# Wv in chunks, x0 in one transfer, the swapped Wv over GpSimd's queue: loads rearranged in a gated mix of linear attention and an MLP

## The chip, the cores and the metric

The kernel runs on one core of one Trainium2 chip. The metric is the device time of one execution in microseconds. Before the change it took 156.04 us (median of 3 runs, 155.99 to 156.21). The span in a profile, from the first to the last instruction, is 1.7 us shorter than the time of the same execution (154.9 us beside 156.61 for the first profile).

## The reference, cut to what matters

x has 2048 rows of 448. One branch is linear attention with 16 heads of 28: q, k and v are projections of x, q and k pass a per-head matrix and a pair of softmaxes, and the products are summed over the sequence. The other branch is a GELU MLP with 1792 hidden units. A sigmoid gate of x mixes both.

```python
g = _sigmoid((x * gate_w).sum(-1, keepdims=True))
qkv = (x @ wqkv) ...                       # wqkv is 448 x 1344: Wq, Wk, Wv side by side
pq = einsum("bhsd,hdf->bhsf", q, w_phi)    # the same for k
phi_q = concat([softmax(pq), softmax(-pq)])
...                                        # kv and z are sums over the sequence; o = num / den
b = einsum("bsf,fd->bsd", gelu(einsum("bsd,df->bsf", x, w1) + b1), w2) + b2
return g * (o @ wo) + (1 - g) * b
```

Of the kernel before, what the change touches and what calls it, by code (L numbers as in the profile page):

```python
# [13 lines left out]
D = 448  # L14
# [3 lines left out]
P = 128  # L18
# [5 lines left out]
NJ = 14  # L24
# [4 lines left out]
HP = 64  # L29
# [6 lines left out]
def kernel(  # L36
# [14 lines left out]
    nc = tc.nc  # L51
    x = A_x[0]
# [16 lines left out]
    def four(name):  # L69
        turn[0] += 1  # L70
        return wide(name) if turn[0] % 4 == 0 else pair(name)
# [26 lines left out]
    WvG = attn.tile([P, NC4, D + 1], BF16, name="WvG")  # L98
    WvS = attn.tile([P, NC4, D + 1], BF16, name="WvS")
# [4 lines left out]
    WkT = attn.tile([P, NG, D], BF16, name="WkT")  # L104
    WqT = attn.tile([P, NG, D], BF16, name="WqT")
    wphi = attn.tile([P, NC4, DH], BF16, name="wphi")
# [4 lines left out]
    b1c = w2_sb[:, 6, 0:P]  # L111
    nc.gpsimd.memset(b1c, 0.0)
    warm = w2_sb[:, 0, 0:P]
    gate = w2_sb[:, 1, :]
# [3 lines left out]
    nc.vector.memset(WvG[0:64, 3, :], 0.0)  # L118
    nc.vector.memset(wo_sb[64:P, 3, :], 0.0)
    nc.vector.memset(Wpk[0:64, 3, :], 0.0)  # L120
    nc.vector.memset(WkT[0:1, 0, 0:1], 0.0)
    wphi_rows = A_w_phi.rearrange("h a b -> (h a) b")
    x0 = oT[:, 0, 0:4 * D].rearrange("p (t d) -> p t d", t=4)
    for m, eng in ((0, nc.scalar), (1, nc.sync)):
        eng.dma_start(x0[:, 2 * m:2 * m + 2, :],
                      x[m * 256:(m + 1) * 256, :].rearrange("(t p) d -> p t d", p=P))
    nc.scalar.dma_start(WvG[:, 0:3, 0:D],
                        A_wqkv[0:384, 2 * D:3 * D].rearrange("(c p) n -> p c n", p=P))
    nc.scalar.dma_start(WvG[64:P, 3, 0:D], A_wqkv[384:448, 2 * D:3 * D])
    nc.sync.dma_start(gate[0:1, :], gate_w[None, :])  # L130
    nc.scalar.dma_start(wphi[:, 0:3, :], wphi_rows[0:384, :].rearrange("(c p) b -> p c b", p=P))

    def load_x(b):
        blk = slice(b * 512, (b + 1) * 512)
        nc.sync.dma_start_transpose(xT[:, 0:3, blk], x[blk, 0:384])  # L135
        nc.sync.dma_start_transpose(xT[:, 3, blk], x[blk, 320:448])  # L136
# [4 lines left out]
    def swap_x(h):  # L141
        ev = slice(2 * h * 512, 2 * h * 512 + 512)
        od = slice(2 * h * 512 + 512, 2 * h * 512 + 1024)
        nc.sync.dma_start(xS[0:HP, :, h, :], xT[HP:P, :, ev])  # L144
        nc.sync.dma_start(xS[HP:P, 0:3, h, :], xT[0:HP, 0:3, od])
# [1 line left out]
    load_wT(WkT, D)  # L147
    load_wT(WqT, 0)
    load_x(1)
    nc.scalar.dma_start(wphi[0:64, 3, :], wphi_rows[384:448, :])  # L150


    first = consts.tile([1, 1], F32, name="first")
# [1 line left out]
    nc.gpsimd.memset(ident[:], 1.0)  # L155
    nc.gpsimd.affine_select(out=ident[:], in_=ident[:], pattern=[[-1, P]],
                            compare_op=ALU.is_equal, fill=0.0, base=0, channel_multiplier=1)
    nc.gpsimd.memset(hmask[:], 1.0)
    nc.gpsimd.affine_select(out=hmask[:], in_=hmask[:], pattern=[[P, NC4], [-DH, H]],
                            compare_op=ALU.is_ge, fill=0.0, base=0, channel_multiplier=1)  # L160
# [14 lines left out]
                          in_=mask[:, PW:PW + 2, None].to_broadcast([P, 2, DH]))  # L175
    nc.gpsimd.memset(KVbd[:], 0.0)
    for g in range(NG):
        nc.gpsimd.tensor_copy(
            out=KVbd[:, g].rearrange("p s (i w) -> p s i w", i=2)[:, :, :, KW - 2:KW],
            in_=m4[:, None, :, :].to_broadcast([P, 2, 2, 2]))  # L180
# [36 lines left out]
    def prep(W_T, out_at, engines):  # L217
        for m in range(2):
            w_ps = four("w_ps")
            for i in range(2):  # L220
                c = 2 * m + i
                dlo = c * P if c < 3 else 320
                for e, (h0, h1) in enumerate(spans):
                    nc.tensor.matmul(w_ps[:, i, h0 * DH:h1 * DH], lhsT=W_T[:, e, dlo:dlo + P],
                                     rhs=bd[:, e, h0:h1, :].rearrange("p h d -> p (h d)"),
                                     start=(e == 0), stop=(e == NC4 - 1), skip_group_check=True)
            src = w_ps[:, :, 0:D].rearrange("p i (x w) -> p i x w", w=PW)
            if m == 0:
                copy(engines[0], out_at(slice(0, P), slice(0, 2)), src)
            else:  # L230
                copy(engines[1], out_at(slice(0, P), 2), src[:, 0])
                copy(engines[2], out_at(slice(HP, P), 3), src[HP:P, 1])
# [108 lines left out]
    def turn_gate():  # L341
        g_ps = four("g_ps")
        for c in range(NC4):
            lo = c * P if c < 3 else 320
            nc.tensor.matmul(g_ps[:, 0, c:c + 1], lhsT=gate[:, lo:lo + P], rhs=ident[:, 0:1],
                             start=True, stop=True)
        nc.scalar.copy(out=WvG[:, 0:3, D], in_=g_ps[:, 0, 0:3])  # L347
        nc.scalar.copy(out=WvG[HP:P, 3, D:D + 1], in_=g_ps[HP:P, 0, 3:4])

    def dummies(n):  # L350
# [8 lines left out]
    turn[0] += 2  # L359
    turn_x0(0, xp[0])  # L360
    turn_gate()
    turn_x0(1, xp[1])
    fill_bd()
# [1 line left out]
    v_pair(1)  # L365
    prep(WkT, wk_at, (1, 0, 1))
    prep(WqT, wq_at, (1, 0, 0))
    def swap_w(W_S, W):
        nc.sync.dma_start(W_S[0:HP, :, :], W[HP:P, :, :])  # L369
        nc.sync.dma_start(W_S[HP:P, 0:3, :], W[0:HP, 0:3, :])  # L370

    nc.sync.dma_start(b1c[0:NJ, :], B_b1.rearrange("(j p) -> j p", p=P))
    load_x(2)
    swap_w(WqS, Wpq)
    swap_x(0)
    load_x(3)
    swap_w(WkS, Wpk)
    swap_x(1)
    swap_w(WvS, WvG)
    for f in (slice(0, F // 2), slice(F // 2, F)):  # L380
        for i in range(2):
            nc.sync.dma_start(w1_sb[i * HP:(i + 1) * HP, :, f],
# [163 lines left out]
```

## The kernel before: what the change touches

The first 512 rows of x (x0) are turned on TensorE; the other three blocks come transposed by the DMA. Wv carries the gate's weights as one more column (WvG). From the second half of the sequence on, TensorE runs two half-height matmuls at once. For that the kernel needs copies with the two partition halves swapped: xS of x, WqS, WkS and WvS of the weights. Each is an on-chip copy by DMA.

```python
nc.vector.memset(WkT[0:1, 0, 0:1], 0.0)      # holds the transposed load of WkT back
for m, eng in ((0, nc.scalar), (1, nc.sync)):
    eng.dma_start(x0[:, 2 * m:2 * m + 2, :], x[m * 256:(m + 1) * 256, :].rearrange(...))
nc.scalar.dma_start(WvG[:, 0:3, 0:D], A_wqkv[0:384, 2 * D:3 * D].rearrange(...))
nc.scalar.dma_start(WvG[64:P, 3, 0:D], A_wqkv[384:448, 2 * D:3 * D])
nc.sync.dma_start(gate[0:1, :], gate_w[None, :])
# ... wphi; then on SyncE: WkT, WqT, load_x(1)
```

The order on SyncE's queue, once Wq and Wk are prepared, and TensorE's order beside it:

```python
nc.sync.dma_start(b1c[0:NJ, :], B_b1.rearrange("(j p) -> j p", p=P))   # b1
load_x(2); swap_w(WqS, Wpq); swap_x(0)
load_x(3); swap_w(WkS, Wpk); swap_x(1)
swap_w(WvS, WvG)
# ... then w1, wo, b2, w2
k_pair(0); k_pair(1); k_norm(0); k_pair(2); v_pair(2); k_norm(1)
k_pair(3); v_pair(3, b1=True)                # its last matmul turns b1
for g in range(NG): q_pair(g, 0)             # needs WqS and xS of the first half
for r in range(4):                           # needs WkS, xS of the second half, then WvS
    k_two(r); v_two(r); k_norm(4 + r); q_pair(r, 1)
```

The softmax here doesn't subtract the row's maximum and nothing guards it: scores larger than these inputs give would overflow.

## Time and profile before

| | before |
|---|---|
| time | 156.04 us |
| span of the profiled execution | 154.9 us |
| TensorE busy | 149.4 us, 96% |
| granted TensorE clock | 0.998 |
| mean DMA rate from 1 to 20 us | 199 GB/s |

The prediction below shows the busy shares, the chain, the holes in TensorE's timeline and the first waits. Two rows of the page of 40 equal slices (3.9 us each; a digit is the busy share in tenths) complete them, for TensorE and for the DMA engines:

```profile
PE   7799999999999999999999999999999999999991
DMA  5999999999995000000000001114332123334401
```

TensorE is full from the third slice on. The DMA row is at 9 in slices 2 to 12, that is from 4 to 46 us. Averaged over whole slices, both are busy at once there. A 9 does not mean that the DMA engines are never idle: this share can exceed 1 (it is 4.01 from 14.5 to 15 us, at 108 GB/s).

### The profile page before, as it was taken

Reading aid. Unit: us, or ns where it says so; the run is one execution under the profiler, and the core shown is the slowest. Engines: PE = TensorE matmul, PEld = TensorE weight load, DVE = VectorE, ACT = ScalarE, POOL = GpSimd, SP = SyncE. Lnnn points to the kernel's source line nnn. Section 1 sums busy time; section 2 is a strip of 40 time slices with the busy share of each in tenths; the row PEclk is TensorE's granted clock in tenths of the full one; section 3 lists DMA queues with packets and bytes.
Section 4 is the critical chain, followed back from the end, with each engine's and each line's share of the span. In section 5 each row is a group of like instructions: output and inputs, shape, how many; then the busy total and the mean of one; then the engine's idle time right before and its main releaser. Section 6 shows DMA issues by size and latency. Waiting matters only on the chain.

```text
span 154.9 us, 3180 instructions
## 1 busy us (share of the span) xinstructions
PE 149.4 (96%) x1302; PEld 83.8 (54%) x1302; DVE 83.2 (54%) x246; ACT 77.1 (50%) x90; POOL 31.8 (21%) x34
## 2 busy tenths in 40 slices
PE   7799999999999999999999999999999999999991
PEld 2475545566666864444444455555556555555581
DVE  3444999288892050000000049999977999977100
ACT  0659759998889626777767650111311111111121
POOL 7900489919776000000000000000000000000000
PEclk9999999999999999999999999999999999999999
DMA  5999999999995000000000001114332123334401
GB/s 147 255 199 146 190 235 248 221 221 212 213 336 176 4 0 4 0 0 4 0 0 0 4 0 34 34 38 96 86 101 64 40 64 90 81 85 37 122 31 30
DMA packets 28270, 14.91 MB, mean 96 GB/s; under 512 B 20062, under 2 KB 27872, under 8 KB 28256
## 3 DMA queue, kind: packets, MB, share of 16 engines
q1 hardware_dynamic: 27024, 14.06, 42.0%
q10 hardware_dynamic: 1232, 0.66, 1.5%
q8 instruction: 10, 0.16, 0.5%
q14 instruction: 4, 0.03, 0.1%
HBM read 6.11 MB, written 1.84 MB: 51 GB/s over the span
## 4 chain that ended last, share of the span: by engine, by line
PE 79%; SPq 13%; DMA 3%; issue 1%; DVE 1%; ACT 0%; ACTq 0%
PE y L485 27%; PE hp L426 27%; PE y L491 8%; PE nm L441 4%; PE pq L307 4%; PE v_ps L291 4%; SPq L135 3%; SPq L139 3%; SPq L136 3%; DMA WvS<-WvG 3%; PE pk L299 3%; PE acc L318 2%; SPq L369 1%; SPq L370 1%; SPq L144 1%
## 5 line engine op out<-in xcount | busy, mean ns | idle before, releaser
L485 PE MATMUL y<-w_sb,gel 128*128 128x448 bf16 (+1 forms) x238 | 45.2, 341 | 0.0
L426 PE MATMUL hp<-xT,w_sb 64*128 64x512 bf16 x196 | 42.6, 376 | 0.0
L426 PE MATMUL hp<-xS,w_sb 64*128 64x512 bf16 x196 | 42.3, 376 | 0.0
L431 ACT ACTIVATE gel<-hp,b1T 128x1024 bf16<-128x1024 f32 x28 | 30.8, 1111 | 13.0 <-PE hp L426 13.0
L494 ACT ACTIVATE res<-y,ungate 128x448 bf16<-128x448 f32 (+1 forms) x17 | 10.4, 612 | 50.4 <-PE y L491 50.2
L485 PEld LDWEIGHTS <-gel 128*128 128x128 bf16 x238 | 23.1, 98 | 19.0
L426 PEld LDWEIGHTS <-w_sb 64*128 64x128 bf16 x392 | 20.5, 94 | 21.6
L268 POOL TENSOR_TENSOR phik<-phik,rec 128x1792 bf16<-128x1792 bf16 (+1 forms) x8 | 25.0, 3129 | 16.1 <-DVE rec L265 16.1
L446 DVE COPY st<-nm 128x32 f32<-128x32 f32 x32 | 4.5, 184 | 35.5 <-PE nm L441 35.5
L462 DVE TENSOR_TENSOR tmp<-nm,al 128x448 bf16<-128x448 f32 x32 | 18.4, 617 | 0.0
L263 DVE TENSOR_REDUCE sums<-phik 128x64 f32<-128x1792 bf16 x8 | 16.0, 2006 | 2.6 <-ACT phik L256 2.6
L491 PE MATMUL y<-wo_sb,oT 128*128 128x448 bf16 (+1 forms) x68 | 14.7, 341 | 0.0
L307 PE MATMUL pq<-xT,Wpq 64*128 64x512 bf16 x56 | 13.2, 376 | 0.0
L307 PE MATMUL pq<-xS,WqS 64*128 64x512 bf16 x56 | 11.5, 376 | 0.1
L196 DVE CAST vaug<-v_ps 128x896 bf16<-128x896 f32 x7 | 7.5, 1074 | 6.0 <-PE v_ps L291 3.6
L312 ACT ACTIVATE EqP<-pq 128x1024 bf16<-128x1024 f32 x8 | 8.3, 1041 | 3.7 <-PE pq L307 3.7
L313 ACT ACTIVATE EqN<-pq 128x1024 bf16<-128x1024 f32 x8 | 8.3, 1042 | 0.0
L441 PE MATMUL nm<-KVbd,EqP 128*128 128x120 bf16 x64 | 8.3, 216 | 0.0
L441 PE MATMUL nm<-KVbd,EqN 128*128 128x120 bf16 x64 | 8.3, 216 | 0.0
L255 ACT ACTIVATE phik<-pk 128x896 bf16<-128x896 f32 x8 | 7.5, 940 | 1.4 <-PE pk L277 1.4
L491 PEld LDWEIGHTS <-oT 128*128 128x128 bf16 x68 | 6.1, 98 | 3.3
L208 PE MATMUL v_ps<-WvG,xT 128*128 128x449 bf16 x32 | 6.6, 354 | 1.0 <-ACT WvG L347 1.0
(90 smaller groups left out, 145.7 us busy)
## 6 DMA issues: line engine op xcount, KB each, us to landing
w_sb<-in_B_w_dram SPq DMA_DIRECT2D x4, 784.0 KB, 14.2
out_dram<-res SPq DMA_DIRECT2D x15, 112.0 KB, 1.9
w_sb<-in_B_w_dram SPq DMA_DIRECT2D x1, 1568.0 KB, 17.3
xS<-xT SPq DMA_DIRECT2D x2, 256.0 KB, 4.0
xS<-xT SPq DMA_DIRECT2D x2, 192.0 KB, 4.3
WvG<-in_A_wqkv_dram ACTq DMA_DIRECT2D x1, 336.0 KB, 4.5
wo_sb<-in_A_wo_dram SPq DMA_DIRECT2D x1, 336.0 KB, 17.0
WqS<-Wpq SPq DMA_DIRECT2D x1, 256.0 KB, 4.6
```

The lines of the kernel that those rows point to most:

```text
L263: nc.vector.reduce_sum(out=sums[:], in_=ph, axis=AX.X)
L268: eng.tensor_tensor(out=ph[:, lo:hi], in0=ph[:, lo:hi], in1=rec[:, lo:hi, :, None].to_broadcast([P, hi - lo, 2, DH]), op=ALU.mult)
L307: nc.tensor.matmul(pq[:, i, :], lhsT=w_half(Wpq, WqS, i, k)[:, g * P:(g + 1) * P], rhs=x_half(i, k, h), start=(k == 0), stop=(k == NK - 1))
L312: nc.scalar.activation(out=EqP[:, g, dst], in_=src, func=ACT.Exp)
L313: nc.scalar.activation(out=EqN[:, g, dst], in_=src, func=ACT.Exp, scale=-1.0)
L426: nc.tensor.matmul(hp[:, i, :], lhsT=w1_sb[i * HP:(i + 1) * HP, k, j * P:(j + 1) * P], rhs=x_half(i, k, h), start=(k == 0), stop=(k == NK ...
L431: nc.scalar.activation(out=gel[h][:, j, :], in_=hp[:].rearrange("p a b -> p (a b)"), func=ACT.Gelu_apprx_tanh, bias=b1T[:, j:j + 1])
L441: nc.tensor.matmul(nm[s][:, g * 2 * KW:(g + 1) * 2 * KW], lhsT=E[:, g, tok], rhs=KVbd[:, g, s, :], start=True, stop=True)
L462: nc.vector.tensor_tensor(out=tmp[:, s, :].rearrange("p (x h d) -> p x h d", x=NPR, h=2), in0=nmv[s][:, :, 0:PW].rearrange("p x (h d) -> p ...
L485: nc.tensor.matmul(y, lhsT=gel[t // 8][:, j, (t % 8) * P:(t % 8 + 1) * P], rhs=w2_sb[:, j, cols], start=(j == 0), stop=False)
L491: nc.tensor.matmul(y, lhsT=oT[:, c, tok], rhs=wo_sb[:, c, cols], start=False, stop=(c == NC4 - 1))
L494: nc.scalar.activation(out=res[:, cols], in_=y, func=ACT.Copy, scale=ungate[:, t:t + 1])
```

## The change

Its intent: let the first value matmul start as soon as its piece of Wv is there, and take the two long copies of the swapped Wv, and a small load, off SyncE's and ScalarE's queues. The diff, cut to its core:

```diff
-    nc.vector.memset(WkT[0:1, 0, 0:1], 0.0)
-    for m, eng in ((0, nc.scalar), (1, nc.sync)):
-        eng.dma_start(x0[:, 2 * m:2 * m + 2, :], ...)
-    nc.scalar.dma_start(WvG[:, 0:3, 0:D], ...)
+    nc.scalar.dma_start(x0, x[0:512, :].rearrange("(t p) d -> p t d", p=P))
+    nc.sync.dma_start(gate[0:1, :], gate_w[None, :])
+    for c, eng in ((0, nc.sync), (1, nc.scalar), (2, nc.sync)):
+        eng.dma_start(WvG[:, c, 0:D], A_wqkv[c * P:(c + 1) * P, 2 * D:3 * D])
...                                  # wphi's last 64 rows: ScalarE's queue -> GpSimd's
-        nc.scalar.copy(out=WvG[:, 0:3, D], in_=g_ps[:, 0, 0:3])
+        for c in range(3):
+            nc.scalar.copy(out=WvG[:, c, D:D + 1], in_=g_ps[:, 0, c:c + 1])
...
-    nc.sync.dma_start(b1c[0:NJ, :], B_b1.rearrange("(j p) -> j p", p=P))
+    swap_w(WvS, WvG, nc.gpsimd)
     load_x(2)
     swap_w(WqS, Wpq)
     swap_x(0)
+    nc.sync.dma_start(b1c[0:NJ, :], B_b1.rearrange("(j p) -> j p", p=P))
     load_x(3)
     swap_w(WkS, Wpk)
     swap_x(1)
-    swap_w(WvS, WvG)
```

More of the change, by code (lines that the diff above doesn't have):

```diff
@@ L120 @@
     nc.vector.memset(Wpk[0:64, 3, :], 0.0)
-    nc.vector.memset(WkT[0:1, 0, 0:1], 0.0)
     wphi_rows = A_w_phi.rearrange("h a b -> (h a) b")
     x0 = oT[:, 0, 0:4 * D].rearrange("p (t d) -> p t d", t=4)
-    for m, eng in ((0, nc.scalar), (1, nc.sync)):
-        eng.dma_start(x0[:, 2 * m:2 * m + 2, :],
-                      x[m * 256:(m + 1) * 256, :].rearrange("(t p) d -> p t d", p=P))
-    nc.scalar.dma_start(WvG[:, 0:3, 0:D],
-                        A_wqkv[0:384, 2 * D:3 * D].rearrange("(c p) n -> p c n", p=P))
+    nc.scalar.dma_start(x0, x[0:512, :].rearrange("(t p) d -> p t d", p=P))
+    nc.sync.dma_start(gate[0:1, :], gate_w[None, :])
+    for c, eng in ((0, nc.sync), (1, nc.scalar), (2, nc.sync)):
+        eng.dma_start(WvG[:, c, 0:D], A_wqkv[c * P:(c + 1) * P, 2 * D:3 * D])
     nc.scalar.dma_start(WvG[64:P, 3, 0:D], A_wqkv[384:448, 2 * D:3 * D])
-    nc.sync.dma_start(gate[0:1, :], gate_w[None, :])
     nc.scalar.dma_start(wphi[:, 0:3, :], wphi_rows[0:384, :].rearrange("(c p) b -> p c b", p=P))
@@ L149 @@
     load_x(1)
-    nc.scalar.dma_start(wphi[0:64, 3, :], wphi_rows[384:448, :])
     first = consts.tile([1, 1], F32, name="first")
@@ L157 @@
                             compare_op=ALU.is_equal, fill=0.0, base=0, channel_multiplier=1)
+    nc.gpsimd.dma_start(wphi[0:64, 3, :], wphi_rows[384:448, :])
     nc.gpsimd.memset(hmask[:], 1.0)
@@ L367, with swap_w @@
     prep(WqT, wq_at, (1, 0, 0))
-    def swap_w(W_S, W):
-        nc.sync.dma_start(W_S[0:HP, :, :], W[HP:P, :, :])
-        nc.sync.dma_start(W_S[HP:P, 0:3, :], W[0:HP, 0:3, :])
-    nc.sync.dma_start(b1c[0:NJ, :], B_b1.rearrange("(j p) -> j p", p=P))
+    def swap_w(W_S, W, eng=nc.sync):
+        eng.dma_start(W_S[0:HP, :, :], W[HP:P, :, :])
+        eng.dma_start(W_S[HP:P, 0:3, :], W[0:HP, 0:3, :])
+    swap_w(WvS, WvG, nc.gpsimd)
     load_x(2)
```

## The prediction

> **What bounds the kernel now.** I read the page's busy shares first, then the chain that ended last, then the waits, then the timelines of TensorE (PE, and PEld for its weight loads) and of SyncE's queue (SPq) over the first 30 us, and last a table of short windows for the DMA engines.
>
> ```profile
> PE 149.4 (96%) x1302; PEld 83.8 (54%) x1302; DVE 83.2 (54%) x246; ACT 77.1 (50%) x90; POOL 31.8 (21%) x34
> ```
>
> PE works for 149.4 of 154.9 us, so at most 5.5 us of the span are no PE work. The change removes no PE instruction. It can only win what PE loses between its instructions in the part that the change touches, and the diff touches only loads and copies that are done before 31 us. The 40-slice row says the same: PE is at 9 from the third slice to the last but one.
>
> The chain shows SyncE's queue for 13%, which looks like a bigger lever than it is:
>
> ```profile
> 23.47 0.94 SPq L369
> ...
> 24.46 4.13 DMA WvS<-WvG
> 28.59 0.04 issue
> 28.63 1.49 PE v_ps L291 x13
> ```
>
> It walks back from the last output through PE to 28.63 us, and there it leaves PE for the queue of transfers (WvS is the half-swapped copy of Wv; L369 and L370 issue it). That does not mean that PE was idle before: it had been at work from 6.32 us. What PE lost at this joint is in its own timeline:
>
> ```profile
> 28.05 0.35 PE L299 MATMUL pk<-Wpk,xT 64*128 64x448 bf16 x1
> 28.23 0.35 PE L291 MATMUL v_ps<-WvG,xT 64*128 64x449 bf16 x1
> ...
> 28.63 0.37 PE L291 MATMUL v_ps<-WvS,xS 64*128 64x449 bf16 x2
> 28.82 0.37 PE L291 MATMUL v_ps<-WvG,xT 64*128 64x449 bf16 x2
> ```
>
> These matmuls start every 0.19 us; after 28.23 the next was due at 28.42 and came at 28.63. **WvS costs 0.21 us.** The same reading finds a second joint:
>
> ```profile
> 20.55 0.39 PE L307 MATMUL pq<-xT,Wpq 64*128 64x512 bf16 x1
> 21.06 0.39 PE L307 MATMUL pq<-xS,WqS 64*128 64x512 bf16 x2
> 21.27 0.39 PE L307 MATMUL pq<-xT,Wpq 64*128 64x512 bf16 x2
> ```
>
> Spacing 0.215, so 21.06 was due at 20.77: **0.29 us** lost. The view puts no name on it ("issue"); the operand that came last should be xS (swapped copy of x), since its second half is issued at 16.46 and such copies take a median 4.3 us to land, that is about 20.8. The third joint is the start:
>
> ```profile
> PE v_ps L208 <- ACT WvG L347: 1.0, 1, 1.0
> ACT WvG L347 <- DMA WvG<-in_A_wqkv_dram: 1.0, 1, 1.0
> PEld L208 <- DVE xT L196: 0.8, 1, 0.8
> PEld L337 <- DMA oT<-in_A_x_dram: 0.8, 1, 0.8
> ```
>
> Read from the bottom: the transposes of x0 wait for its load until 4.10 (which costs nothing, as seven warm-up matmuls run until 4.16). Then two things are awaited at once. The first weights of the value matmuls wait for the copy of xT and load at 5.91. The matmul waits for the gate column in WvG, written by ScalarE at 6.10 because that write waits for the one large load of Wv, and starts at 6.32. So of the 1.04 us of idle PE only 6.32 less about 6.00 belongs to Wv, **0.32 us**; the rest belongs to the x0 path. The three joints hold 0.32 + 0.29 + 0.21 = 0.82 us, the most that this change can win.
>
> **What the Trainium skill says.** "DMA: Bandwidth & Descriptors", section "Issuing engines are not separate DMA queues": transfers from any engine share the same 16 DMA engines, and another issuer saves only the issue time. Here issue time is real: the two WvS copies hold SyncE's queue for 0.94 and 0.75 us. Same page, "Rules for kernel authors": merge small transfers, and two halves issued apart do not run faster than one. That speaks for one x0 transfer and against splitting Wv for bandwidth; the trace agrees that the engines are the limit early (share 0.92 and 249 GB/s in 2 to 3 us, 1.10 and 348 GB/s in 3 to 4 us). "SBUF — State Buffer", section "SBUF: two separate sides": VectorE in a two-port mode can keep GpSimd from writing descriptors. No transfer of this trace comes from GpSimd, so it does not show it. "TensorE: Matmul & The Clock Gate", section "What's actually happening": an idle window of some 3.4 us halves the clock; the granted clock here is 0.998 and the gaps are far shorter.
>
> **The change, part by part.**
>
> *Wv per chunk, gate per chunk.* One load of three chunks becomes three (two from SyncE, one from ScalarE), and the gate write becomes three one-column writes. I take it that the old write waited because its span of addresses crosses the load's, and that the new ones no longer do; then ScalarE does four copies of about 0.17 us at about 5.1 to 5.8 (the gate's matmuls end at 4.81, ScalarE is free at 5.11), ahead of the 6.00 when xT allows. Its xT copy for the second half also moves up from 6.47 to about 5.9. Value: up to 0.32 us, if the chunks have landed by 6.0.
>
> *x0 in one transfer.* 448 KB on ScalarE's queue, no longer 224 KB on each of two. The bytes are the same, but two Wv chunks (224 KB) now share the engines with it from SyncE's queue from about 1.2 us. By 4.0 us the engines had moved about 11 + 249 + 348 = 608 KB (the one-microsecond windows from 1 to 4 us); x0 and two chunks are 672 KB, so x0 may land up to 0.2 to 0.3 us later. It lies on the path (transposes, xT copy, first matmul). And the first transposes now wait for all of x0. Cost: 0.2 us as an estimate.
>
> *The WkT memset is gone.* It held SyncE's transposed weight loads until 2.65. With the gate load (0.35) and two chunks (0.46 each, as x0's half took) plus gaps, they begin at about 2.2: **0.45 us earlier**. The load of b1 (0.49 + 0.05) also moves behind the xS copies, so the second x block is issued about 1.0 us earlier, at 9.7. The swapped Wq waits for Wpq, done at 12.77, so it is issued at about 12.85 rather than 13.59, and xS at 15.75 rather than 16.46. With 0.7 us in hand the 0.29 us at 20.77 should go.
>
> *WvS over GpSimd.* GpSimd ends its setup at 8.0 us (plus about 1 us for the small w_phi copy put into it) and stands idle until 17.55, so its issue is free. The copies, 224.5 + 168.4 KB, then run at about 9 to 13 us and land over 10 us before 28.4: the 0.21 us goes. SyncE's queue gets 0.94 + 0.75 us back, so the MLP weights come that much sooner; nothing waits for them now, so that is worth nothing.
>
> Sum: 0.32 + 0.29 + 0.21 - 0.20 = 0.62 us. I take off another 0.1 for contention and for a queue more to set up: **155.5 us**.
>
> **Rivals.** (1) *The swapped Wv collides with x.* 393 KB at some 230 GB/s is 1.7 us of the DMA engines, just where the second and third blocks of x arrive. Against it: there is room,
>
> ```profile
> 11.50:12.00 0.50, 0.50 (x4) 0.26 (x3) 0.50 (x1) 0.47 (x2) 0.00 (x0) 1.00 0.15 30
> 12.00:12.50 0.50, 0.50 (x5) 0.23 (x3) 0.49 (x2) 0.50 (x1) 0.00 (x0) 1.00 0.62 98
> 15.00:16.00 1.00, 1.00 (x7) 0.50 (x6) 1.00 (x1) 1.00 (x2) 0.00 (x0) 1.00 0.27 16
> ```
>
> The last but one column is the share of the DMA engines in use: 0.43 + 0.19 + 0.73 = 1.35 us of them stand idle in these three windows. The second block, issued at 7.20 and 8.74 with a median 4.5 us to landing, is there at about 13.2 and is needed at about 14.3 (the key matmuls begin at 11.28 and take 1.52 for each pair of tiles). For the rival: the room is a little less than the need, and the old order kept these copies late. If it holds, PE waits 0.3 to 0.8 us at 14.3 or again at xS, and the time is about 156.1 to 156.6.
>
> (2) *x0 becomes the bound of the start.* If the single transfer lands at 4.8 rather than 4.1, every step to the first value matmul moves by 0.7 us, and of the 0.32 us nothing is left: 156.04 + 0.7 - 0.32 - 0.29 - 0.21, about 155.9. For it: all the bytes are now waited for at once, with Wv beside them. Against it: the early rate is high and Wv was beside it before.
>
> (3) *GpSimd's set-up slips.* The small w_phi copy stands ahead of the head mask, which the block-diagonal weights need at 6.30 (mask done at 2.28, so 4 us of room), and its rows must be there for the fourth of those products at about 7.1; it is issued near 1.5. If it took 6 us, the weight preparation at 9.4 would still have most of its slack. I expect nothing, within 0.1 us.
>
> (4) *All transfers were hidden anyway*, and another operand arrives just as late as the one freed: then 156.0.
>
> **Range and chances.** The best sum without any cost is 156.04 - 0.82 = 155.2, and 154.7 if xS or the start hide a bit more than I could read from the spacing. Rival 1 at its worst gives 156.6. So 154.7 to 156.6, with 155.5 in its better half, as three of the four costs have slack in the trace. A gain of over 2% is a time under 152.9, 3.1 us less; all the idle PE in the touched stretch is under 2 us. A loss of over 2% is above 159.2, and would need a stall that no operand here is close to. Faster 0.02, same 0.96, slower 0.02.
>
> **What would show it.** Right: in the waits, ScalarE's gate write no longer waits for Wv, and the first value matmul starts by about 6.2; SyncE's first transposed load is issued near 2.2; in PE's timeline the q matmuls run on without the 0.29 us hole and the swapped value matmuls without the 0.21 us hole; the chain no longer goes through WvS; PE's busy time stays at 149.4 and the span falls by about 0.6. Wrong: a PE or weight-load wait for x0 later than 4.4 (rival 2); a new wait at the third pair of key tiles or a later xS (rival 1); DMA windows from 9 to 13 us full and x landing later than before. The prediction fails if GpSimd's copies delay the transfers that PE waits for by more than the 0.7 us that SyncE's queue has gained, or if the clock's warm-up moves because PE idles longer before 6 us.

## The result, and the profile after

The changed kernel took 158.07 us (157.83 to 158.33, 4 runs) beside 156.08 us (155.99 to 156.21) for the kernel before on the same chip: a ratio of 1.0127, with a 95% interval of 1.0109 to 1.0145. It is slower, by 2.0 us; the predicted range ended at 156.6. Ratios here and below are the mean time of one kernel's fast runs over that of the other's in the same rounds, so not quite the ratio of the medians. Executions over 1.5% slower than the fastest of the same kernel are left out of the means.

Line numbers moved: the value matmul L208 is now L205, the b1 matmul L211 is L208, the key matmul L277 is L274, the q matmul L307 is L304, the block load of x (L135, L136) is L132, L133. The page of the changed kernel, the same two rows:

```profile
PE   7999959999999999999999999999999999999991
DMA  4999999999993000000000001116342123334401
```

TensorE has a 5 in its sixth slice, 19.6 to 23.5 us: a new hole. The view of waits (engine, line, what it waited for: us in total, times, longest) names it:

```profile
PEld L208 <- DMA w_sb<-in_B_b_dram: 2.3, 1, 2.3
PE v_ps L208 <- DMA w_sb<-in_B_b_dram: 1.8, 1, 1.8
...
PEld L274 <- DMA xT<-in_A_x_dram: 0.7, 1, 0.7
```

The first two lines are the b1 matmul. It stands in TensorE's stream ahead of the q matmuls, and the change had moved its load behind the swapped x. TensorE's timeline shows what follows (start, length, operation):

```profile
22.52 0.18 PE L208 MATMUL v_ps<-ident,w_sb 128*128 128x14 bf16 x1 [1.83 <-DMA w_sb<-in_B_b_dram]
22.63 0.39 PE L304 MATMUL pq<-xT,Wpq 64*128 64x512 bf16 x1
22.63 0.60 PE L304 MATMUL pq<-xS,WqS 64*128 64x512 bf16 x2
```

The q matmuls begin at 22.63 instead of 20.55. The hole of 0.29 us before the swapped ones is gone, but only because everything they need has landed while TensorE stood still. This looks like a plain blunder with b1. But it is worth looking one step back, at SyncE's queue. Before:

```profile
10.66 1.45 SPq L135 DMA_TRANSPOSE xT<-in_A_x_dram  x1
...
16.46 0.62 SPq L145 DMA_DIRECT2D xS<-xT  x1
```

and after:

```profile
10.26 2.56 SPq L132 DMA_TRANSPOSE xT<-in_A_x_dram  x1
...
17.02 0.60 SPq L142 DMA_DIRECT2D xS<-xT  x1
17.66 1.07 SPq L374 DMA_DIRECT2D w_sb<-in_B_b_dram  x1
```

The third block of x was issued 0.4 us earlier but its issue took 2.56 us, not 1.45, and the swapped x that the prediction expected at 15.75 went out at 17.02. SyncE's first transposed load, which the prediction had 0.45 us earlier, went out at 2.58 us instead of 2.65. So x itself is late, and b1 may only stand in front of it. That called for experiments.

### The profile page after: what moved, and what is told of

Same layout as the page of the kernel before. It is cut to its first block, busy times and chain, and to the rows that moved or that the text cites. A ratio compares the mean times of both kernels' runs of the same rounds, so it can differ in the third digit from the quotient of the medians.

```text
span 156.4 us, 3187 instructions
## 1 busy us (share of the span) xinstructions
PE 149.9 (96%) x1302; PEld 80.4 (51%) x1302; DVE 83.3 (53%) x245; ACT 77.4 (50%) x92; POOL 33.8 (22%) x37
## 4 chain that ended last, share of the span: by engine, by line
PE 83%; SPq 10%; DMA 3%; issue 1%; ACT 0%; DVE 0%; ACTq 0%
PE hp L424 27%; PE y L483 27%; PE pq L304 8%; PE y L489 8%; PE nm L439 4%; PE v_ps L288 3%; PE pk L296 3%; DMA w_sb<-in_B_b_dram 3%; SPq L132 3%; SPq L136 3%; PE acc L315 2%; SPq L133 2%; SPq L368 1%; SPq L126 1%; SPq L141 0%
## 5 line engine op out<-in xcount | busy, mean ns | idle before, releaser
L424 PEld LDWEIGHTS <-w_sb 64*128 64x128 bf16 x392 | 19.0, 94 | 23.0
L265 POOL TENSOR_TENSOR phik<-phik,rec 128x1792 bf16<-128x1792 bf16 (+1 forms) x8 | 25.0, 3128 | 15.5 <-DVE rec L262 15.5
L304 PE MATMUL pq<-xT,Wpq 64*128 64x512 bf16 x56 | 12.9, 376 | 0.0
L304 PE MATMUL pq<-xS,WqS 64*128 64x512 bf16 x56 | 12.9, 376 | 0.0
L252 ACT ACTIVATE phik<-pk 128x896 bf16<-128x896 f32 x8 | 7.6, 946 | 1.7 <-PE pk L274 1.6
L253 ACT ACTIVATE phik<-pk 128x896 bf16<-128x896 f32 x8 | 7.6, 952 | 0.0
## 6 DMA issues: line engine op xcount, KB each, us to landing
w_sb<-in_B_w_dram SPq DMA_DIRECT2D x1, 1568.0 KB, 16.6
```

The lines of the kernel that those rows point to most:

```text
L265: eng.tensor_tensor(out=ph[:, lo:hi], in0=ph[:, lo:hi], in1=rec[:, lo:hi, :, None].to_broadcast([P, hi - lo, 2, DH]), op=ALU.mult)
L304: nc.tensor.matmul(pq[:, i, :], lhsT=w_half(Wpq, WqS, i, k)[:, g * P:(g + 1) * P], rhs=x_half(i, k, h), start=(k == 0), stop=(k == NK - 1))
L424: nc.tensor.matmul(hp[:, i, :], lhsT=w1_sb[i * HP:(i + 1) * HP, k, j * P:(j + 1) * P], rhs=x_half(i, k, h), start=(k == 0), stop=(k == NK ...
```

## The experiments

Theory A: the late b1 alone costs the time. Theory B: the swapped Wv, moved forward, takes engine time from loads that TensorE needs sooner, and b1 only covers them. Further rivals came up on the way: C, GpSimd's queue costs of itself; D, the new order of the first loads costs. B1 and B2 in the expectations are theory B in sharper words: the early bytes cost, whichever queue carries them.

**The kernel before once more**, with no edit, for the spread.

> The kernel before, unchanged, for a second profile and to see the spread. Both theories: 156.1 us, ratio 1.000 within 0.001. The first profile of it was of an execution of 156.6 us, 0.5 above the median; if the 0.29 us hole before the swapped q matmuls and the 0.21 us hole before the swapped value matmuls are smaller or gone here, then the gain that the prediction counted for those two was not there in a median execution.

Measured: 156.48 us beside 156.38, ratio 1.0002 (0.9983 to 1.0021). In its profile the swapped q matmuls have a hole of 0.13 us (20.94 where 20.81 was due; 0.29 in the first profile) and the swapped value matmuls one of 0.19 (28.49 where 28.30 was due; 0.21 in the first). So the holes are real, but the first differs from one execution to the next by as much as half of what the prediction meant to win there. The first value matmul started at 6.36 us here.

**b1 back in its old place**, in the changed kernel.

```diff
     swap_w(WvS, WvG, nc.gpsimd)
+    nc.sync.dma_start(b1c[0:NJ, :], ...)
     load_x(2)
     swap_w(WqS, Wpq)
     swap_x(0)
-    nc.sync.dma_start(b1c[0:NJ, :], ...)
```

> The changed kernel with the load of b1 back in its old place, ahead of the third block of x on SyncE's queue. Theory A (the late b1 alone costs the time: the b1 matmul stands ahead of the q matmuls on PE and waits for it): the 1.83 us wait of the b1 matmul goes, about 155.9 us. Theory B (the swapped Wv over GpSimd crowds the DMA engines and holds SyncE's transposes, so that the swapped x is late as well, hidden behind b1): PE now waits for the swapped x at the first q matmuls, which is issued another 0.5 us later, landing at about 22.1 where 20.8 is due: about 157.3 us.

Measured: 157.98 us over its five fast runs (a sixth, of 160.42, was slow) beside 156.38, ratio 1.0110 (1.0089 to 1.0132). Theory A's 155.9 is out. Theory B had expected 157.3 and a wait for the swapped x; the loss is larger and its longest wait lies even earlier, at the block of x itself.

```profile
PE pk L274 <- DMA xT<-in_A_x_dram: 1.8, 1, 1.8
...
PE w_ps L221 <- DMA WqT<-in_A_wqkv_dram: 0.6, 1, 0.6
...
PE pk L296 <- DMA xS<-xT: 0.3, 1, 0.3
```

**b1 among the first loads on ScalarE's queue**, with SyncE's order as in the change.

```diff
+    nc.scalar.dma_start(b1c[0:NJ, :], ...)      # right behind wphi's first load
...
-    nc.sync.dma_start(b1c[0:NJ, :], ...)        # behind swap_x(0)
```

> The changed kernel with the load of b1 on ScalarE's queue among the first loads, so that SyncE's order stays as in the changed kernel. Theory A: no wait for b1 and none in its place, about 155.9 us. Theory B: the first q matmuls wait for the swapped x, issued at 17.0 and landing at about 21.6 where 20.8 is due: about 156.9 us.

Measured: 158.09 us, ratio 1.0127 (1.0103 to 1.0150): just the loss of the change, with no wait for b1 at all, and 1.2 us above what theory B had expected. The wait is now for the swapped x:

```profile
PE pq L305 <- DMA xS<-xT: 0.8, 1, 0.8
```

The edit also did something unmeant: ScalarE issued this fifth load at 4.17 us only, and the first value matmul started at 6.37 us instead of 5.99. That late start doesn't explain the loss, as TensorE waits later on for the swapped x.

**b1 late, alone, in the kernel before.**

```diff
-    nc.sync.dma_start(b1c[0:NJ, :], ...)
     load_x(2)
     swap_w(WqS, Wpq)
     swap_x(0)
+    nc.sync.dma_start(b1c[0:NJ, :], ...)
```

> The kernel before with nothing changed but the load of b1, moved behind the first swapped x as in the change. Theory A: b1 is issued at about 16.6 and lands about 4.8 us later, at 21.4, where 20.44 is due: a wait of about 0.9 us at the b1 matmul, part of it in place of the hole at the q matmuls, so 156.7 to 157.0 us. Theory B: without the GpSimd copies the queue is shorter and b1 is nearly in time: within 0.3 us of the kernel before.

Measured: 156.20 us beside 156.38, ratio 1.0002 (0.9977 to 1.0027). TensorE waits 0.27 us for b1 and has no hole at the q matmuls: one took the other's place. Theory A falls on all three counts. The wait for b1 in the changed kernel was the last of several late arrivals, not their cause.

**The swapped Wv over GpSimd, alone, in the kernel before.**

```diff
+    swap_w(WvS, WvG, nc.gpsimd)      # ahead of load_x(2), issued at about 8 us
...
-    swap_w(WvS, WvG)                 # last on SyncE's queue
```

> The kernel before with nothing changed but the two copies of the swapped Wv, moved to GpSimd's queue at about 8 us. Theory B1 (393 KB moved ahead of loads that PE waits for, 1.7 us of the DMA engines): x or its swapped copy lands 1 to 2 us later and PE waits for it, 157.4 to 158.1 us. Theory D (the new order of the first loads delays the transposed loads, the swapped Wv is innocent): within 0.3 us of the kernel before.

Measured: 157.45 us beside 156.37, ratio 1.0080 (1.0057 to 1.0103). This one part carries most of the loss. TensorE waits for x at the key matmuls (0.5 us) and for the swapped x at the q matmuls (1.1 us):

```profile
PE pq L307 <- DMA xS<-xT: 1.1, 1, 1.1
...
PE pk L277 <- DMA xT<-in_A_x_dram: 0.5, 1, 0.5
```

**The first loads, alone** (x0 in one transfer, Wv and gate per chunk, no memset).

> The kernel before with only the first part of the change: x0 in one transfer, Wv in chunks with the gate column per chunk, no memset ahead of the transposed loads; b1, the small w_phi load and the swapped Wv stay as before. Theory B1: a gain of 0 to 0.3 us at the first value matmul, nothing lost, so 155.9 to 156.4 us. Theory D: 157.4 us or more.

Measured: 156.70 us beside 156.37, ratio 1.0024 (1.0011 to 1.0036). Theory D is out as the main cause; but a small loss, not a gain, is there. The run doesn't hold this part quite as the change has it. The small w_phi load stayed on ScalarE's queue here and was issued at 4.23 us (3.06 in the kernel before), so ScalarE wrote the gate columns from 6.13 us (5.33 in the changed kernel), and the first value matmul started at 6.32, no earlier than before.

**The change with the swapped Wv back on SyncE's queue**, everything else as in the change.

```diff
-    swap_w(WvS, WvG, nc.gpsimd)
...
     swap_x(1)
+    swap_w(WvS, WvG)
```

> The changed kernel with only the swapped Wv put back on SyncE's queue at its old place; b1 late and the small w_phi copy on GpSimd stay. Theory B1: the loss goes, 155.9 to 156.4 us (the late b1 alone cost nothing in the run before). Theory D: stays at about 158 us.

Measured: 156.41 us beside 156.37, ratio 1.0014 (0.9992 to 1.0035). Undoing this one part takes the loss away, with b1 late and the small load on GpSimd still in place.

**The swapped Wv early on SyncE's queue**, without GpSimd.

```diff
     nc.sync.dma_start(b1c[0:NJ, :], ...)
+    swap_w(WvS, WvG)
     load_x(2)
...
-    swap_w(WvS, WvG)
```

> The kernel before with the swapped Wv issued first on SyncE's queue, between b1 and the third block of x, at about 10.7 us instead of 23.5, so the same early bytes without GpSimd. Theory B1 (the early bytes cost): the third block of x and the swapped x are issued 1.8 us later and land 1.5 to 2 us later, about 157.8 us. Theory C (it is GpSimd's own queue, which takes its share of every engine beside the transposes instead of waiting its turn, that costs): the copies fill idle room, and what is lost is less than 0.8 us: below 156.9.

Measured: 157.58 us beside 156.37, ratio 1.0087 (1.0073 to 1.0100). The loss is as large without any GpSimd transfer. Its TensorE timeline at the q matmuls:

```profile
20.36 0.39 PE L307 MATMUL pq<-xT,Wpq 64*128 64x512 bf16 x1
22.15 0.39 PE L307 MATMUL pq<-xS,WqS 64*128 64x512 bf16 x2 [1.40 <-DMA xS<-xT]
```

The swapped matmuls were due 0.215 us after 20.36 and came 1.79 after it.

**The swapped Wv over GpSimd, late** (behind GpSimd's first normalisation).

```diff
     k_norm(0)
+    swap_w(WvS, WvG, nc.gpsimd)      # issued at 20.5 us
...
-    swap_w(WvS, WvG)
```

> The kernel before with the swapped Wv on GpSimd's queue, but behind GpSimd's first normalisation, so issued at about 21 us rather than 9. Theory B1 (it is the early place of the 393 KB that costs, whichever queue carries them): within 0.4 us of the kernel before, 156.0 to 156.8. Theory C (GpSimd's queue costs of itself, by descriptors or by its share beside the transposes): 157.0 us or more, as in the run with the early GpSimd copies (1.1 us above the kernel before).

Measured: 158.00 us beside 156.47, ratio 1.0093 (1.0070 to 1.0116). The theory as I had put it missed this. The q matmuls no longer wait, but the key matmuls of the second half do:

```profile
PE pk L299 <- DMA xS<-xT: 1.1, 1, 1.1
```

At 20.5 us the second half's copies of Wk and x were only just being issued (20.06 to 23.7 us). So this place was still ahead of copies that are needed first, or GpSimd's queue does cost of itself. The run below tries the same place without GpSimd.

**The swapped Wv on SyncE's queue ahead of the swapped Wk**, the same late place without GpSimd.

```diff
     load_x(3)
+    swap_w(WvS, WvG)
     swap_w(WkS, Wpk)
     swap_x(1)
-    swap_w(WvS, WvG)
```

> The kernel before with the swapped Wv on SyncE's queue ahead of the swapped Wk (at about 20.7 us, where the late GpSimd copy was issued), no GpSimd transfer. Theory B2 (bytes that overtake what PE needs sooner cost it, whichever queue): PE waits 1.0 to 1.7 us for the swapped x of the second half at the key matmuls near 27.5 us, nothing at the value matmuls: 157.3 to 158.1 us. Theory C (GpSimd's queue costs of itself): within 0.5 us of the kernel before.

Measured: 157.70 us beside 156.51, ratio 1.0072 (1.0055 to 1.0089), and the same wait for the same operand:

```profile
26.65 0.35 PE L299 MATMUL pk<-Wpk,xT 64*128 64x448 bf16 x1
28.29 0.36 PE L299 MATMUL pk<-WkS,xS 64*128 64x448 bf16 x2 [1.29 <-DMA xS<-xT]
```

No queue of GpSimd's is needed for the loss, at either place. What the four runs share is that Wv's bytes went ahead of others that TensorE needs sooner. What holds those others back is not the same in the traces: over GpSimd's queue the transposed loads take longer to land (a median of 5.7 us from their issue in the early run, 4.7 before; in the late run it is the swapped x, up to 5.6 us, 4.6 before), while on SyncE's queue they land as fast (4.4) but are issued later, as the two copies' own issue (1.15 us early, 1.18 us late) stands ahead of them. One account by bytes covers all four; two separate costs of like size, one for each queue, are not excluded.

**Half the dose**: only the smaller copy (168 of 393 KB) early over GpSimd.

```diff
+    nc.gpsimd.dma_start(WvS[HP:P, 0:3, :], WvG[0:HP, 0:3, :])   # ahead of load_x(2)
...
-    swap_w(WvS, WvG)
+    nc.sync.dma_start(WvS[0:HP, :, :], WvG[HP:P, :, :])
```

> A dose: only the smaller of the two swapped Wv copies (168 of 393 KB) goes early over GpSimd, the other stays at its old place on SyncE's queue. Theory B1, bytes: about 168/393 of the 1.1 us, so 0.4 to 0.7 us above the kernel before. If the room that the windows showed (1.35 us of idle engines) takes the smaller copy whole, as the prediction assumed for both: no more than 0.2 us.

Measured: 156.88 us beside 156.47, ratio 1.0020 (1.0002 to 1.0038). By bytes, 0.43 of 0.80% would be 0.34%; the interval holds that as well as the 0.13% of the other view. The loss is smaller than with the whole; how it grows with the bytes stays open. The two issues of the third block of x took 2.74 us together here, about as before (2.71), while they took 3.48 to 4.57 us in the six profiles with all of Wv early, on either queue.

**The change once more**, on the chip of the runs above it.

> The changed kernel again, on the chip of the parts. Sum of the parts measured alone: first loads 0.24%, swapped Wv early 0.80%, late b1 0.02%: 1.06% or 1.7 us above the kernel before, 158.0 us. If it is 2.0 us or more above, the parts make each other worse; the copy of w_phi over GpSimd was in no run alone.

Measured: 157.86 us over its five fast runs (a sixth, of 160.26, was slow) beside 156.47, ratio 1.0109 (1.0076 to 1.0141). The parts measured alone add up to 1.06%. Nothing beyond their sum is shown.

**Two attempts at something faster.** If the order of the bytes must stay, the order of TensorE's work can move instead. Both runs keep the kernel before, put b1 late, and let each q pair of the second half go ahead of the value pair, so that WvS is needed 1.5 us later.

```diff
 for r in range(4):
     k_two(r)
-    v_two(r)
-    k_norm(4 + r)
     q_pair(r, 1)
+    v_two(r)
+    k_norm(4 + r)      # first attempt: k_norm ahead of q_pair
```

> An attempt to beat both kernels without moving bytes forward: the kernel before with b1 late (free in its own run) and, on PE, each q pair of the second half ahead of the value pair, so that the swapped Wv is needed 1.5 us later. Theory B1: the 0.2 us hole before the swapped value matmuls goes, at most 0.3 us gained, 155.9 to 156.3 us; nothing worse.

Measured: 157.85 us beside 156.47, ratio 1.0091 (1.0074 to 1.0109), a miss. With the normalisation first, VectorE reached the emptying of the value pair's tile in PSUM (the memory that the matmuls write to) late, and TensorE waited for the tile:

```profile
PEld L426 <- DVE lg L196: 1.4, 1, 1.4
...
PE hp L426 <- DVE lg L196: 0.9, 1, 0.9
```

> As e11 (b1 late, q pairs of the second half ahead of the value pairs), but the normalisation behind the value pair in program order, so that VectorE empties the PSUM tiles first, which e11 was seen to wait for. Theory B2: the 0.2 us hole before the value matmuls goes and nothing new is waited for: 155.9 to 156.4 us, at most 0.3 us better than the kernel before. If PE waits for VectorE again: above 157.

Measured: 156.23 us beside 156.51, ratio 0.9976 (0.9959 to 0.9994). A small gain, clear of 1: the best version, and 1.3 to 1.5% below the change by the ratios (0.9976 over 1.0109 or 1.0127). Key, q and value matmuls follow each other without the hole in front of the swapped ones. The interval is a gain of 0.1 to 0.6 us; that hole was 0.2 us.

## Why the prediction was wrong, point by point

**The bound.** That TensorE is the bound and that only its holes can be won was right: TensorE's busy time is 149.9 us after the change, and what was lost is waiting. What the reading left out is that several loads arrive only just in time: two of the three small holes are waits of 0.1 to 0.3 us in front of swapped copies, and every run that put all of Wv ahead of these or of x had a longest wait of 0.8 to 1.8 us there or, in the changed kernel, at the b1 matmul just ahead. I read the holes as losses to be won one by one.

**The step that failed** is the one under "WvS over GpSimd": "The copies, 224.5 + 168.4 KB, then run at about 9 to 13 us and land over 10 us before 28.4: the 0.21 us goes." That hole did go. But the copies were booked as free, apart from 0.1 us for contention, because 1.35 us of idle engine time stood against their 1.7 us; in the runs they cost 1.1 to 1.4 us. They landed at about 13.6 and 16.6 us, the second 7.1 us after its issue. The windows from 1 to 20 us test that room (the last two columns are the share of the DMA engines in use and GB/s). Before:

```profile
1.00:20.00 19.00, 17.90 (x121) 9.90 (x122) 10.86 (x21) 11.99 (x18) 8.86 (x23) 1.00 1.04 199
```

and after:

```profile
1.00:20.00 19.00, 18.68 (x121) 10.32 (x122) 10.71 (x21) 12.23 (x19) 11.15 (x26) 1.00 1.08 206
```

In 19 us that is 3.78 MB before and 3.91 MB after. Of the 0.40 MB that were put in front, only 0.13 MB were extra; the other 0.27 MB stands for loads behind them that had not yet moved. At the 235 GB/s that the changed kernel moves from 20 to 24 us this is an estimate of 1.1 us (0.9 to 1.4 with the other profiles, whose rates over the same 19 us are 199 and 200 GB/s without and 204 to 209 with the early Wv), the size of what the early swapped Wv cost alone (157.45 and 157.58 us beside 156.37). The idle share in three short windows was not room to be filled: idle time is still there after the change, from 15.5 to 16.5 us, while the swapped x is about to be issued (16.27 and 17.02):

```profile
15.50:16.00 0.50, 0.50 (x5) 0.26 (x3) 0.50 (x1) 0.50 (x1) 0.00 (x0) 1.00 0.05 5
16.00:16.50 0.50, 0.50 (x4) 0.24 (x3) 0.50 (x1) 0.43 (x2) 0.00 (x0) 1.00 0.11 16
```

So the runs show that the copies delayed what stood behind them, and not that the engines' time ran out. What limits the supply at these moments was not taken apart and stays open.

**Rival 1** (the copies collide with x) was what happened, and had been named; its size was wrong. It was given 0.3 to 0.8 us and a worst time of 156.6. The early Wv alone cost 0.80% and 0.87%, 1.1 to 1.4 us, in its two places, and the whole change 2.0 us. The prediction's own condition for failing, that the copies delay transfers by more than the 0.7 us gained on SyncE's queue, is what came about.

**The gain on SyncE's queue** did not come. "With 0.7 us in hand the 0.29 us at 20.77 should go": the swapped x was issued at 17.02, not 15.75. I had moved issue times forward with their old lengths, but the issue of a transposed load did not keep its length beside the early copies: the third block's first half took 2.56 us instead of 1.45. Nor did the transposed weight loads start 0.45 us earlier without the memset (2.58 beside 2.65 us). The Trainium skill, "DMA: Bandwidth & Descriptors", section "Queues, rings and completion order", says that each DMA engine takes turns between the queues that have work for it; GpSimd's copies beside SyncE's transposes fit that, but the equal loss without GpSimd shows that sharing between queues is not needed for a loss.

**b1** was taken for a load that can move at will. Its matmul is in TensorE's stream ahead of the q matmuls, and the timeline of the kernel before has it at 20.44 us, one line above those that the prediction showed. In the changed kernel it was the wait that showed, 1.83 us; it was not the cause, as three runs say.

**The first loads** went about as told in the traces and not in the times. Over ten profiles with the old first loads the first value matmul starts at 5.96 to 6.63 us, mean 6.27; over six with the new ones at 5.70 to 6.37, mean 6.02. The six are of two kinds: where ScalarE has a fifth load to issue (b1 first, and this part alone) they are 6.37 and 6.32, and in the other four 5.70 to 6.03, mean 5.86. That is 0.41 us gained, where 0.32 less 0.20 had been counted, and in these profiles it is there only where that queue has four loads, as in the change. The transposes of x0 start at 4.12 us in the mean of the ten and at 4.21 in the mean of the six, so its one transfer cost about 0.1, not 0.2. Yet alone this part made the kernel 0.24% slower: TensorE waits 0.4 us for the swapped x in that profile. Which of its pieces does it, the chunks ahead of the transposed loads, the missing memset or the late w_phi load, was not taken apart and stays open.

**Rivals 2 and 3** did not occur: x0 did not become the bound, and the small w_phi load over GpSimd (in no run alone) is part of the version that is within 0.14% of the kernel before. Rival 4, another operand just as late behind the one freed, is what the runs on b1 showed.

## What to carry to other kernels

Where loads arrive only just in time, a transfer that is issued early was not free in any of the four places tried: it goes ahead of something, so keep the transfers in the order in which the bound engine needs them, whatever queue they are on. When a profile shows one late load, first ask what stands behind it: move it away in an experiment and see whether another wait takes its place. Small holes in front of several operands in a row can be a sign that the whole supply is only just in time, and there reordering the consumer can win a little (0.24% here) where reordering the loads lost.

## What the Trainium skill lacked or had wrong

- "DMA: Bandwidth & Descriptors", section "Rules for kernel authors", advises to issue a DMA early and wait on it late. It lacks the condition that no load stands behind it that is needed sooner: 393 KB moved forward by some 15 us over GpSimd's queue cost 0.80%, by 13 us on SyncE's 0.87%, and by only 3 us still 0.93% and 0.72%.
- The same page, section "Issuing engines are not separate DMA queues", says that another issuer saves only issue time. Here the two copies' 1.69 us of issue were taken off SyncE's queue, and the loads behind them went out only 0.57 us earlier (24.68 us instead of 25.25), as the issue of a transposed load stretched from 1.45 to 2.56 us. No page that I read gives a size for this stretching.
- "Perfetto Trace Analysis", section "Identifying the Most-Contended Engine", calls the occupancy of the DMA engines misleading. It lacks that a low share in a short window need not be usable room: 1.35 us stood idle before, and only 0.13 of 0.40 MB more were moved.
